# Float32 array tiles for z, scores and reads, with w_in kept in SBUF, in a fused attention and feed-forward kernel on Trainium2

## The chip, the core and the metric

The kernel runs on one core of one Trainium2 chip. The metric is device time in microseconds (us) of one execution. Before the change it was run three times: 707.71, 709.49 and 711.24 us, median 709.49 us. The profile shows one execution on core 0 whose span, from the first to the last instruction, is 706.6 us.

## The reference

Eight batches b, eight heads, 512 tokens (S), 32 states (N), head width 64 (D). Each batch is attended both ways, the two results are laid one after the other (544 rows of 512 columns), and all rows go through a feed-forward layer without gate (512 to 2048 to 512). All in float32.

```python
scores = scale * np.matmul(x, state.transpose(0, 1, 3, 2))      # 512 x 32 per head
a = softmax(scores)                                             # exp, / (sum + 1e-9)
xread = np.matmul(a, state)
scores2 = scale * np.matmul(state, x.transpose(0, 1, 3, 2))     # 32 x 512 per head
a2 = softmax(scores2)
sread = np.matmul(a2, x)
x = concat([xread, sread], axis=2)     # then tokens x (heads * 64)
h = x @ w_in
r = np.maximum(h, 0.0)
g = r * r
out = g @ w_out
```

## The kernel before, in words

The token rows need `h = a @ state @ w_in`. The kernel never forms `a @ state`; it forms `z = state @ w_in` for each head (32 states by 2048 columns), so that eight heads of 32 states make 256 rows, two groups (g = 0, 1) of 128, and `h` is a sum over these 256 rows. The state rows (`sread`) are collected over all batches in `sr` and go through the layer at the very end in a run of their own.

Full precision on the fast matrix path is had by splitting: `split` writes a rounded `hi` (type F32R, by ACT) and `lo = src - hi` (by DVE or POOL), and a product is the sum of hi*hi, lo*hi and hi*lo. A matmul whose operands are plain F32 needs no split; in the trace it is two MATMUL records for one instruction of the program.

The feed-forward layer runs in units. A unit is one 128-column piece `fc` (of 16) of the 2048 middle columns for one batch: `up(fc)` is 6 matmuls 128x512 into `ph` (line L392), then ACT takes relu (L394), DVE or ACT squares it (L398, L396), and the result is split to `g_hi`, `g_lo`; `down` is 12 matmuls 128x512 into `po` (L418), two units later. 8 batches x 16 pieces are 128 units; the state rows add 16 short units of width 256. `BOTH` sets their order: six pieces of batch 0, ten of batch 1, then the rest of both, then batches 2 to 7 whole.

Both weight matrices arrive as 64-bit words. `singles` makes float32 of them: one ACT operation (L108) and three DVE operations (L109, L113, L117) per 128x512. `wo_load` splits w_out into resident `wo_hi`, `wo_lo` (the lo part on POOL). A part of w_in (`z_part.load`, `convert`) is converted to `wf`, written to DRAM (`wd`), split (`cut`) and used for the z of four batches at once (`product`, the states of batches 0 to 3 as 128 columns): six parts by plain F32 matmuls (L191), where head pairs sit in partitions 0 to 63 and 64 to 127, the others by F32R matmuls (L203). ACT copies z out of PSUM (`z_stage`) and sends it to DRAM (`zd`); `z_fetch` brings one batch's 256 columns back by four transfers (`z_raw`, L230) and splits them to `z_hi`, `z_lo`. For batches 4 to 7 the parts of w_in are read back from `wd`. At the end the state rows read w_in from `wd` again (`wi_raw`, L624).

Attention of a batch is done in two groups of four heads: `load_t`, `cut_t`, `scores` (L288 with split operands into `pq`; L298 with plain F32 into `pst` for batches 0 and 1), a softmax along the 32 states after a DVE transpose (`soft1`, `soft1b`), and for the state rows an exp along the tokens (`e2`, L309), PE transposes (`turn`, L343), and `read` (L355).

The order of steps around the units is set by two lists (`weights`, `reads`) with due slots; each unit calls `aux` twice, and steps are taken at a rate that meets the due slots. The tile framework's scheduler then orders the instructions of each engine. PE, ACT, DVE and POOL each run their own instructions in that order; SP and ACT issue the transfers.

Of the kernel before, what the change touches and what calls it, by code (L numbers as in the profile page):

```python
# [9 lines left out]
F32 = mybir.dt.float32  # L10
# [8 lines left out]
def memory_attention_then_relu2_ffn(  # L19
# [4 lines left out]
    stT: bass.AP,  # L24
# [19 lines left out]
    B, C, S = xT.shape  # L44
    D = stT.shape[1]
# [9 lines left out]
    FW = 256  # L55
    NFCH = DF // FW
    FPC = FW // P
# [5 lines left out]
    RAW = 4  # L63
    XRAW = 2
    PLAIN_Z = 6
    PLAIN_X = 2
    BOTH = ((0, 6), (1, 10), (0, NFC), (1, NFC))
    LATE = 3

    def pool_early(early):  # L70
        return nc.gpsimd if early else nc.vector
# [3 lines left out]
    dr = ctx.enter_context(tc.tile_pool(name="dr", bufs=1, space=bass.MemoryType.DRAM))  # L75
# [6 lines left out]

    wo = [None] * NFCH
    sp_hl = const.tile([P, NG, 2, 2, 2 * N], F32R, name="sp_hl")
    nc.gpsimd.memset(sp_hl.bitcast(F32), 0.0)
    sp_f = const.tile([P, NG, 2, P + D], F32, name="sp_f")
    nc.gpsimd.memset(sp_f, 0.0)
    sr = [const.tile([P, C], F32, name=f"sr{i}") for i in range(NGB)]

    wd = [dr.tile([P, NCC, FW], F32, name=f"wd_{k}") for k in range(NFCH)]  # L90
    zd, st, z_first = {}, {}, []
    for G in range(NGB):
        for k in range(NFCH):
            zd[G, k] = dr.tile([P, NG, HG, FW], F32, name=f"zd_{G}_{k}")

# [27 lines left out]
    def z_state(G):  # L123
        if G == 0:
            raw = sb.tile([P, H, GB * N], F32, name="st_f", tag="x_hl", bufs=1)
            st["raw"] = raw
        else:
            raw = sb.tile([P, H, GB * N], F32, name="st_raw", tag="raw", bufs=RAW)
        for j in range(2):
            nc.sync.dma_start(out=raw[j * D:(j + 1) * D].rearrange("d h m -> d (h m)"), in_=stT[G])  # L130
        hi = sb.tile([P, H, GB * N], F32R, name="stz_hi", bufs=1)
        lo = sb.tile([P, H, GB * N], F32R, name="stz_lo", bufs=1)
        if G:
            split(hi, lo, raw, nc.gpsimd)
        else:
            for i in range(2):
                own = slice(i * D, (i + 1) * D)
                other = slice((1 - i) * D, (2 - i) * D)
                for v in (hi, lo):
                    nc.gpsimd.memset(v[other, i::2, :].bitcast(F32), 0.0)  # L140
                split(hi[own, i::2, :], lo[own, i::2, :], raw[own, i::2, :], nc.vector)
        st[G] = hi, lo

    def z_part(G, k, g):

        box = {}
        ccs = slice(g * NCC // NG, (g + 1) * NCC // NG)
        nq = NCC // NG

        def load():  # L150
            if G:
                box["wf"] = sb.tile([P, nq, FW], F32, name="wf", bufs=2)
                nc.sync.dma_start(out=box["wf"], in_=wd[k][:, ccs, :])
                return
            raw = sb.tile([P, nq, FW, 2], I32, name="w_raw", tag="raw", bufs=RAW)
            nc.sync.dma_start(out=raw.rearrange("p c f w -> p (c f w)"), in_=w_in[k * NG + g])
            box["raw"] = raw

        def convert():
            wf = sb.tile([P, nq, FW], F32, name="wf", bufs=2)  # L160
            singles(wf, box["raw"])
            nc.sync.dma_start(out=wd[k][:, ccs, :], in_=wf)
            box["wf"] = wf

        plain = G == 0 and k * NG + g < PLAIN_Z

        bank = dict(pool=ps_o, tag="po") if G == 0 and k == 0 else dict(pool=ps_x, tag="px")

        def cut():
            if plain:  # L170
                return
            wf = box["wf"]
            w2 = [sb.tile([P, nq, FW], F32R, name=f"w2_{i}", bufs=2) for i in range(2)]
            box["w2"] = w2
            if G == 0:
                split(w2[0], w2[1], wf, nc.vector)
                return
            for i, w in enumerate(w2):
                own = slice(i * D, (i + 1) * D)
                other = slice((1 - i) * D, (2 - i) * D)  # L180
                nc.scalar.copy(out=w[own], in_=wf[own])  # L181
                nc.gpsimd.tensor_sub(out=w[other], in0=wf[own], in1=w[own].bitcast(F32))  # L182

        def product(i):
            def run():
                own = slice(i * D, (i + 1) * D)
                pz = bank["pool"].tile([P, nq, FW], F32, name="pz", tag=bank["tag"])
                for q in range(nq):
                    h = g * HG + 2 * q + i
                    if plain:  # L190
                        nc.tensor.matmul(  # L191
                            pz[:, q, :], lhsT=st["raw"][own, h, :], rhs=box["wf"][own, q, :],
                            start=True, stop=True,
                        )
                        continue
                    st_hi, st_lo = st[G]
                    u, v = (w[:, q, :] for w in box["w2"])
                    todo = ((st_lo, u), (st_hi, u), (st_hi, v))
                    if G:
                        w = box["w2"][i][:, q, :]  # L200
                        todo = (st_lo, w), (st_hi, w)
                    for j, (a, w) in enumerate(todo):
                        nc.tensor.matmul(  # L203
                            pz[:, q, :], lhsT=a[:, h, :], rhs=w,
                            start=j == 0, stop=j == len(todo) - 1,
                        )
                if G == 0 and k == 0:
                    if g == 0 and i == 0:
                        z_first.append(sb.tile([P, NG, FW], F32, name="z_raw", bufs=2))
                    for q in range(nq):  # L210
                        at = (2 * q + i) * N
                        dst = z_first[0][at:at + N, g, :]
                        nc.scalar.copy(out=dst, in_=pz[:N, q, :])
                stage = sb.tile([P, nq, FW], F32, name="z_stage", bufs=3)
                nc.scalar.copy(out=stage, in_=pz)
                dst = zd[G, k].rearrange("p g (q i) f -> p g q i f", i=2)[:, g, :, i, :]
                nc.scalar.dma_start(out=dst, in_=stage)
            return run

        return load, convert, cut, [product(i) for i in range(2)]  # L220

    def z_fetch(b, k):
        if k or b:
            raw = sb.tile([P, NG, FW], F32, name="z_raw", bufs=2)
        at = (b % GB) * N
        if (b, k) == (0, 0):
            raw = z_first[0]
        else:
            for j in range(HG):
                nc.sync.dma_start(  # L230
                    out=raw[j * N:(j + 1) * N], in_=zd[b // GB, k][at:at + N, :, j, :]
                )
        hi = sb.tile([P, NG, FW], F32R, name="z_hi", bufs=2)
        lo = sb.tile([P, NG, FW], F32R, name="z_lo", bufs=2)
        split(hi, lo, raw, nc.vector)
        return hi, lo


    def attention(b):
        pair = []  # L240

        def pad():
            pair.extend(sb.tile([P, NG, S], F32R, name=n, bufs=2) for n in ("a_hi", "a_lo"))
            raw = sb.tile([P, NG, 2, N], F32, name="sp_raw", bufs=2)
            nc.sync.dma_start(out=raw.rearrange("p g q n -> p (g q n)"), in_=stP[b])
            for i in range(2):
                rows = slice(i * D, (i + 1) * D)
                at = slice(i * N, (i + 1) * N)
                if b < PLAIN_X:
                    nc.scalar.copy(out=sp_f[rows, :, :, at], in_=raw[rows])  # L250
                    continue
                split(sp_hl[rows, :, :, 0, at], sp_hl[rows, :, :, 1, at], raw[rows], nc.vector)

        return pair, pad, [attention_group(b, g, pair) for g in range(NG)]

    def attention_group(b, g, pair):
        CG = C // NG
        NQ = CG // P
        NJ = S // 32
        my = {}  # L260

        def load_t():
            my["t"] = sb.tile([P, NQ, S], F32, name="xt_raw", tag="xraw", bufs=XRAW)
            nc.sync.dma_start(
                out=my["t"], in_=xT[b, g * CG:(g + 1) * CG, :].rearrange("(q p) s -> p q s", p=P)
            )

# [6 lines left out]
        def cut_t():  # L274
            if b < PLAIN_X:
                return
# [228 lines left out]
    for _, _, c, ps in zs[0] + zs[1]:  # L505
        lags[ps[0]] = [(c, 2)]
# [171 lines left out]
```

## Time and profile before

| | |
|---|---|
| three runs | 707.71, 709.49, 711.24 us (median 709.49) |
| the profiled execution | span 706.6 us on core 0; its own time with what lies around the span is not recorded apart, and the median run is 2.9 us above this span |
| busy | PE 669.8, DVE 452.2, ACT 398.3, POOL 199.3 us |
| mean granted TensorE clock | 0.973 |
| transfers | 90.58 MB, HBM read 60.03 MB, written 29.88 MB |

The span divides in two. Up to about 125 us DVE converts the weights, the transfer engines are busy for eight to nine tenths, and PE waits between pieces and is at times granted half its clock. From 125 us on PE is busy nearly without a gap until the last outputs leave. A busy PE is not by that a PE at its peak: durations of single matmuls overlap, and the distance from one start to the next is what one costs in a row of them.

### The profile page before, as it was taken

How to read it: one execution, taken by the hardware profiler on the slowest of the kernel's cores; microseconds unless marked ns; L12 is line 12 of the kernel's file. 1: busy time of each engine (PE TensorE's matmuls, PEld its weight loads, DVE VectorE, ACT ScalarE, POOL GpSimd, SP SyncE). 2: the span in 40 equal slices, each digit the busy share in tenths (PEclk: the TensorE clock that was granted, in tenths of full speed). 3: DMA queues.
4: the chain of work that ended last, by engine and by line, in shares of the span. 5: the costliest groups of instructions: out<-in, count | busy, mean ns of one | idle time of the engine just before them, and what ended most of it. 6: DMA issues, size and time to landing. Idle time of an engine off the chain costs nothing.

```text
span 706.6 us, 9753 instructions
## 1 busy us (share of the span) xinstructions
PE 669.8 (95%) x3152; PEld 551.6 (78%) x3152; DVE 452.2 (64%) x757; ACT 398.3 (56%) x727; POOL 199.3 (28%) x181
## 2 busy tenths in 40 slices
PE   4688789999999999999999999999999999999997
PEld 2355668778888888888888878888888888888996
DVE  4859999758456944447945794797944445443553
ACT  3767687567565863467735653665654344332442
POOL 2314433345443540053403240344242022000000
PEclk8589999999999999999999999999999999999999
DMA  8898899435363542344423312412241112100421
GB/s 276 270 315 283 258 306 315 131 97 153 98 202 122 166 149 62 102 135 120 135 78 120 87 48 74 139 58 90 89 150 61 30 31 90 31 16 0 130 80 32
DMA packets 74548, 90.58 MB, mean 128 GB/s; under 512 B 7680, under 2 KB 57600, under 8 KB 74496
## 3 DMA queue, kind: packets, MB, share of 16 engines
q1 hardware_dynamic: 56896, 72.90, 32.9%
q10 hardware_dynamic: 17600, 17.04, 7.1%
q8 instruction: 25, 0.41, 0.3%
q14 instruction: 27, 0.22, 0.1%
HBM read 60.03 MB, written 29.88 MB: 127 GB/s over the span
## 4 chain that ended last, share of the span: by engine, by line
PE 79%; DVE 8%; DMA 6%; issue 2%; ACT 2%; SPq 1%; POOL 0%; DVEq 0%; ACTq 0%; POOLq 0%
PE po L418 47%; PE ph L392 25%; PE pz L203 3%; DMA wo_raw<-w_out 2%; PE pr L355 2%; DMA sp_raw<-stP 2%; PE pq L288 1%; PE pt L343 1%; DVE wf L117 1%; DVE wf L113 1%; DVE z_lo L98 1%; DVE g_lo L98 1%; DMA zd<-z_stage 1%; DMA xt_raw<-xT 1%; DVE wf L109 1%
## 5 line engine op out<-in xcount | busy, mean ns | idle before, releaser
L418 PE MATMUL po<-wo_hi,g_hi 128*128 128x512 f32 x544 | 217.3, 400 | 0.6 <-ACT g_hi L97 0.5
L418 PE MATMUL po<-wo_lo,g_hi 128*128 128x512 f32 x544 | 215.0, 395 | 0.0
L398 DVE TENSOR_TENSOR ph<-ph,r 128x512 f32<-128x512 f32 (+1 forms) x134 | 89.1, 665 | 169.1 <-ACT r L394 168.9
L394 ACT ACTIVATE r<-ph 128x512 f32<-128x512 f32 (+1 forms) x144 | 82.1, 572 | 171.0 <-PE ph L392 169.6
L418 PE MATMUL po<-wo_hi,g_lo 128*128 128x512 f32 x544 | 152.2, 392 | 0.0
L418 PEld LDWEIGHTS po<-wo_hi,g_hi 128*128 128x128 f32 x544 | 103.9, 191 | 22.4 <-ACT g_hi L97 2.0
L418 PEld LDWEIGHTS po<-wo_lo,g_hi 128*128 128x128 f32 x544 | 103.9, 191 | 19.5
L418 PEld LDWEIGHTS po<-wo_hi,g_lo 128*128 128x128 f32 x544 | 101.5, 189 | 21.1 <-issue 1.0
L98 DVE TENSOR_TENSOR g_lo<-ph,g_hi 128x512 fp32r<-128x512 f32 (+1 forms) x144 | 94.4, 656 | 36.3 <-ACT g_hi L97 27.7
L97 ACT CAST g_hi<-ph 128x512 fp32r<-128x512 f32 (+1 forms) x144 | 81.0, 563 | 57.9 <-DVE ph L398 51.7
L392 PE MATMUL ph<-a_hi,z_hi 128*128 128x512 f32 x256 | 81.4, 399 | 2.6 <-DVE nm L306 1.5
L392 PE MATMUL ph<-a_lo,z_hi 128*128 128x512 f32 x256 | 80.1, 392 | 0.0
L392 PE MATMUL ph<-a_hi,z_lo 128*128 128x512 f32 x256 | 80.0, 394 | 0.0
L98 POOL TENSOR_TENSOR xn_hl<-xn_raw,xn_hl 128x1024 fp32r<-128x1024 f32 x16 | 38.9, 2432 | 138.0 <-ACT xn_hl L97 71.2
L182 POOL TENSOR_TENSOR w<-wf,w 64x512 fp32r<-64x512 f32 x32 | 43.0, 1343 | 74.9 <-ACT w L181 69.8
L392 PEld LDWEIGHTS ph<-a_hi,z_hi 128*128 128x128 f32 x256 | 47.6, 190 | 15.2 <-DVE g_lo L98 2.1
L392 PEld LDWEIGHTS ph<-a_hi,z_lo 128*128 128x128 f32 x256 | 48.5, 190 | 10.4
L392 PEld LDWEIGHTS ph<-a_lo,z_hi 128*128 128x128 f32 x256 | 48.2, 189 | 10.5 <-issue 0.3
L98 POOL TENSOR_TENSOR xt_hl<-xt_raw,xt_hl 128x1024 fp32r<-128x1024 f32 x12 | 28.9, 2406 | 75.4 <-ACT xt_hl L97 43.7
L98 DVE TENSOR_TENSOR z_lo<-z_raw,z_hi 128x512 fp32r<-128x512 f32 x64 | 47.9, 750 | 0.3 <-DMA wd<-wf 0.3
L97 ACT CAST z_hi<-z_raw 128x512 fp32r<-128x512 f32 x64 | 39.2, 615 | 1.3 <-DMA wd<-wf 0.8
L98 POOL TENSOR_TENSOR wo_lo<-wof,wo_hi 128x512 fp32r<-128x512 f32 x16 | 25.2, 1578 | 51.4 <-ACT wo_hi L97 51.4
(97 smaller groups left out, 833.7 us busy)
## 6 DMA issues: line engine op xcount, KB each, us to landing
zd<-z_stage ACTq DMA_DIRECT2D x64, 256.0 KB, 3.2
z_raw<-zd SPq DMA_DIRECT2D x252, 64.0 KB, 2.4
xt_raw<-xT SPq DMA_DIRECT2D x16, 512.0 KB, 3.8
w_raw<-w_in SPq DMA_DIRECT2D x16, 512.0 KB, 5.3
wo_raw<-w_out SPq DMA_DIRECT2D x16, 512.0 KB, 5.8
xn_raw<-xn SPq DMA_DIRECT2D x16, 512.0 KB, 3.9
out<-sum SPq DMA_DIRECT2D x32, 256.0 KB, 2.5
wd<-wf SPq DMA_DIRECT2D x16, 256.0 KB, 3.7
```

Source lines behind the costliest of these rows:

```text
L97: nc.scalar.copy(out=hi, in_=src)
L98: eng_lo.tensor_sub(out=lo, in0=src, in1=hi.bitcast(F32))
L109: nc.vector.tensor_scalar(out=bits, in0=bits, scalar1=3, scalar2=0x7FFFFFF8, op0=ALU.logical_shift_left, op1=ALU.bitwise_and,)
L113: nc.vector.scalar_tensor_tensor(out=bits, in0=high, scalar=-0x80000000, in1=bits, op0=ALU.bitwise_and, op1=ALU.bitwise_or,)
L117: nc.vector.scalar_tensor_tensor(out=bits, in0=low, scalar=29, in1=bits, op0=ALU.logical_shift_right, op1=ALU.bitwise_or,)
L182: nc.gpsimd.tensor_sub(out=w[other], in0=wf[own], in1=w[own].bitcast(F32))
L203: nc.tensor.matmul(pz[:, q, :], lhsT=a[:, h, :], rhs=w, start=j == 0, stop=j == len(todo) - 1,)
L355: nc.tensor.matmul(pr[:, q].rearrange("p i c -> p (i c)"), lhsT=my["e"][:, t, q].rearrange("p i n -> p (i n)"), rhs=my["xn"][:, t, q].rear ...
L392: nc.tensor.matmul(ph, lhsT=w, rhs=v, start=i == 0, stop=i == len(todo) - 1)
L394: nc.scalar.activation(r, ph, AF.Relu)
L398: nc.vector.tensor_mul(out=ph, in0=ph, in1=r)
L418: nc.tensor.matmul(po[t], lhsT=g, rhs=w, start=i == 0 and j == 0, stop=i == last and j == 2)
```

## The change

w_in is converted once into a resident float32 tile `wi` (128 partitions by 4 by 2048: partitions 0 to 63 hold heads 0 to 3, 64 to 127 heads 4 to 7), and stays there; `wd`, `zd`, `z_stage`, `z_raw` and the states of four batches (`stT`) are gone. z of one batch is made when its units come near (`z_piece`): for up to four units at a time, 8 plain F32 matmuls of 64 rows by 32 columns of the array (4 column places j, 2 row halves g), into two PSUM banks; ACT and DVE split the result from PSUM to `z_hi`, `z_lo`. Scores are 8 such matmuls per batch, for all batches, and the result stays in PSUM through both softmaxes. Reads are 32 plain F32 matmuls of 128 rows by 32 columns and 64 wide per batch; the division by the sum moves from `e2` to the 8 small copies into `sr` (DVE). A batch is handled whole, not in two groups, except the softmax of batch 0. `load_w` and `convert_w` work on one queue of 16 pieces of w_in and 16 of w_out, five raw buffers instead of four. The PSUM pool `ps_x` has one buffer of two banks instead of two of one. `BOTH` becomes eight pieces of batch 0, twelve of batch 1, then the rest; `LATE` is 2. POOL keeps `wo_lo`, `a_lo` of batches 1 to 7 and the two softmax operations of batch 1.

```diff
-    RAW = 4
-    PLAIN_Z = 6
-    PLAIN_X = 2
-    BOTH = ((0, 6), (1, 10), (0, NFC), (1, NFC))
-    LATE = 3
+    ZC = 4
+    RAW = 5
+    BOTH = ((0, 8), (1, 12), (0, NFC), (1, NFC))
+    LATE = 2
...
-    ps_x = ctx.enter_context(tc.tile_pool(name="ps_x", bufs=2, space=bass.MemoryType.PSUM))
+    ps_x = ctx.enter_context(tc.tile_pool(name="ps_x", bufs=1, space=bass.MemoryType.PSUM))
...
+    wi = const.tile([P, HG, DF], F32, name="wi")
...
-    def z_part(G, k, g):
-    def z_fetch(b, k):
+    def z_piece(b, units, first):
+        def run():
+            c, at = divmod(units[0], ZC)
...
+            width = len(units) * P
+            cols = slice(units[0] * P, units[0] * P + width)
+            if first:
+                pz = [ps_o.tile([P, S], F32, name=f"pz{g}", tag="po")[:, :width] for g in range(NG)]
+            else:
+                both = ps_x.tile([P, NG, S], F32, name="pz", tag="px")
+                pz = [both[:, g, :width] for g in range(NG)]
+            for j in range(HG):
+                for g in range(NG):
+                    rows = slice(g * D, (g + 1) * D)
+                    nc.tensor.matmul(
+                        pz[g][j * N:(j + 1) * N], lhsT=state[b][rows, j, :],
+                        rhs=wi[rows, j, cols], start=True, stop=True,
+                    )
+            if not first:
+                split(z_hi[:, :, dst], z_lo[:, :, dst], both[:, :, :width], nc.vector)
+                return
...
         def scores():
+            pst = ps_x.tile([P, NG, S], F32, name="pst", tag="px")
+            for j in range(HG):
+                for g in range(NG):
+                    rows = slice(g * D, (g + 1) * D)
+                    nc.tensor.matmul(
+                        pst[j * N:(j + 1) * N, g, :], lhsT=state[b][rows, j, :],
+                        rhs=my["t"][rows, j, :], start=True, stop=True,
+                    )
...
         def read():
+            pr = ps_x.tile([P, NG, S], F32, name="pr", tag="px")
+            for g in range(NG):
+                for t in range(NT):
+                    for j in range(HG):
+                        h = g * HG + j
+                        nc.tensor.matmul(
+                            pr[j * N:(j + 1) * N, g, :D], lhsT=my["e"][:, g, t, j * N:(j + 1) * N],
+                            rhs=my["n"][:, t, h * D:(h + 1) * D], start=t == 0, stop=t == NT - 1,
+                        )
...
+                    nc.vector.tensor_scalar_mul(
+                        sr[b // GB][at:at + N, c:c + D], pr[own, g, :D], my["s2"][own, g:g + 1]
+                    )
...
+    def z_due():
+        while pieces:
+            first, b, cover = pieces[0]
+            if slot[0] < 2 * (first - 2) or ("wi", cover[-1]) in queue[converted[0]:]:
+                break
+            pieces.pop(0)
+            z_piece(b, cover, first < 2)()
...
     def first(fc):
-        raw = sb.tile([P, NCC, P], F32, name="wi_raw", tag="raw", bufs=RAW)
-        nc.sync.dma_start(out=raw, in_=wd[k][:, :, i * P:(i + 1) * P])
...
-        split(w_hi, w_lo, raw, nc.vector)
+        split(w_hi, w_lo, wi[:, :, fc * P:(fc + 1) * P], nc.vector)
```

How the instructions stand, at the places that the prediction speaks of. First PE in the middle of the program. In the order before, z is made in F32R matmuls 128x256 that use the whole array; `w_0` is a part of split w_in, `stz` the split states of four batches, and the rows around are one unit's `up` and `down`.

```order
L418 MATMUL po_2099<-wo_hi_1164,g_lo 128x512
L203 MATMUL pz<-w_0_2888,stz_hi 128x256
L203 MATMUL pz<-w_0_2888,stz_lo 128x256
L418 MATMUL po_2096<-wo_hi_1164,g_hi 128x512
L418 MATMUL po_2096<-wo_lo_1165,g_hi 128x512
L418 MATMUL po_2097<-wo_hi_1164,g_hi 128x512
L418 MATMUL po_2097<-wo_lo_1165,g_hi 128x512
L392 MATMUL ph<-a_hi,z_hi 128x512 x2
```

All of them have the shape of the whole array. Now the same engine in the order after, at a z piece of batch 2 (`sp_raw` is the batch's state, plain F32, and `32x512 x5` are five matmuls with 32 output rows each):

```order
L300 MATMUL po_1670<-wo_hi,g_lo 128x512
L130 MATMUL pz<-wi,sp_raw 32x512 x5
L300 MATMUL po_1667<-wo_hi,g_hi 128x512
L300 MATMUL po_1667<-wo_lo,g_hi 128x512
L300 MATMUL po_1668<-wo_hi,g_hi 128x512
L274 MATMUL ph<-a_hi,z_hi 128x512 x2
```

The other three of that piece's eight stand in the two units that follow, as `L130 MATMUL pz<-wi,sp_raw 32x512 x2` and, 31 rows further on, alone. Counted over the whole order, the 37 pieces of z stand in 55 groups and the 8 scores in 8, with matmuls of full shape in between. The next fence is the last of the three of that piece.

```order
L300 MATMUL po_1670<-wo_hi,g_lo 128x512
L130 MATMUL pz<-wi,sp_raw 32x512
L300 MATMUL po_1667<-wo_hi,g_hi 128x512
L300 MATMUL po_1667<-wo_lo,g_hi 128x512
L300 MATMUL po_1668<-wo_hi,g_hi 128x512
```

A piece that is one step in the code has become three short stretches of PE here.

Then DVE early in the program, up to the eighth `g_lo`, which ends the input of the eighth unit. Before:

```order
L113 SCALAR_TENSOR_TENSOR wof<-wo_raw,wof 128x512
L117 SCALAR_TENSOR_TENSOR wof<-wo_raw,wof 128x512
L98 TENSOR_TENSOR z_lo<-z_raw,z_hi 128x512
L98 TENSOR_TENSOR w_1_985<-wf,w_0_984 128x512
L109 TENSOR_SCALAR wf<-wf 128x512
L113 SCALAR_TENSOR_TENSOR wf<-w_raw,wf 128x512
L117 SCALAR_TENSOR_TENSOR wf<-w_raw,wf 128x512
L98 TENSOR_TENSOR g_lo<-ph,g_hi 128x512
L109 TENSOR_SCALAR wof<-wof 128x512
L98 TENSOR_TENSOR g_lo<-ph,g_hi 128x512
```

Up to here DVE has begun 24 conversions. After, up to the same `g_lo`:

```order
L93 TENSOR_SCALAR wof<-wof 128x512
L97 SCALAR_TENSOR_TENSOR wi<-wi_raw,wi 128x4x128
L82 TENSOR_TENSOR g_lo<-ph,g_hi 128x512
L97 SCALAR_TENSOR_TENSOR wof<-wo_raw,wof 128x512
L101 SCALAR_TENSOR_TENSOR wi<-wi_raw,wi 128x4x128
L101 SCALAR_TENSOR_TENSOR wof<-wo_raw,wof 128x512
L93 TENSOR_SCALAR wi<-wi 128x4x128
L93 TENSOR_SCALAR wof<-wof 128x512
L97 SCALAR_TENSOR_TENSOR wi<-wi_raw,wi 128x4x128
L82 TENSOR_TENSOR g_lo<-ph,g_hi 128x512
```

It has begun 29 of the 32 conversions by then. The splits of w_in (`w_1`) are gone, and z_lo is rarer; conversions have moved into their place.

More of the change, by code (lines that the diff above doesn't have):

```diff
@@ L120, in singles @@
         )
[L123 to L142, printed above, removed]
@@ L144, in z_part @@
-    def z_part(G, k, g):
[L146 to L153, printed above, removed]
-                return
[L155 to L220, printed above, removed]
@@ L222, in z_fetch @@
-    def z_fetch(b, k):
[L223 to L236, printed above, removed]
+    zt = {}
@@ L239, in attention @@
+    state = {}
     def attention(b):
-        pair = []
+        NJ = S // 32
+        pair, my = [], {}
+        halves = [slice(g, g + 1) for g in range(NG)] if b == 0 else [slice(0, NG)]
         def pad():
             pair.extend(sb.tile([P, NG, S], F32R, name=n, bufs=2) for n in ("a_hi", "a_lo"))
[L244 to L260, printed above, removed]
+            state[b] = sb.tile([P, HG, N], F32, name="sp_raw", bufs=3)
+            nc.sync.dma_start(out=state[b].rearrange("p j n -> p (j n)"), in_=stP[b])
         def load_t():
[L263 to L266, printed above, removed]
+            my["t"] = sb.tile([P, HG, S], F32, name="xt_raw", bufs=1)
@@ L282, in scores @@
[L282 to L297 removed]
+            my["n"] = sb.tile([P, NT, C], F32, name="xn_raw", bufs=1)
@@ new lines, in read @@
+            for g in range(NG):
+                for j in range(HG):
+                    c = (j * NG + g) * D
+                    own = slice(j * N, (j + 1) * N)
+                    nc.vector.tensor_scalar_mul(
+                        sr[b // GB][at:at + N, c:c + D], pr[own, g, :D], my["s2"][own, g:g + 1]
+                    )
+        steps = dict(
+            pad=pad, load_t=load_t, scores=scores, exps2=exps2, load_n=load_n, turn=turn, read=read
+        )
+        return pair, steps, [soft(gs) for gs in halves]
@@ L516, in order @@
[L516 to L530 removed]
+        _, w, softs = attentions[b]
@@ new lines, in memory_attention_then_relu2_ffn, with load_next, convert_next @@
+    loaded, converted = [0], [0]
+    def load_next():
+        if loaded[0] < len(queue):
+            load_w(*queue[loaded[0]])
+            loaded[0] += 1
+    def convert_next():
+        convert_w(*queue[converted[0]])
+        converted[0] += 1
+        load_next()
+    pieces = []
+    now = 0
+    for b, fcs in parts:
+        i = fcs[0]
+        while i <= fcs[-1]:
+            new = at[i] == now + i - fcs[0]
+            n = ZC
+            if new:
+                n = 1 if i < 2 else 2
+            cover = range(i, i + n)
+            pieces.append((now + i - fcs[0], b, cover))
+            i += n
+        now += len(fcs)
```

297 lines of the change are left out of this document (114 added, 183 removed).

## The prediction

> **What bounds the kernel now.** I read the engine shares of the page first, then its 40 slices, then the chain that ended last.
>
> ```profile
> PE 669.8 (95%) x3152; PEld 551.6 (78%) x3152; DVE 452.2 (64%) x757; ACT 398.3 (56%) x727; POOL 199.3 (28%) x181
> PE   4688789999999999999999999999999999999997
> DVE  4859999758456944447945794797944445443553
> PEclk8589999999999999999999999999999999999999
> PE 79%; DVE 8%; DMA 6%; issue 2%; ACT 2%; SPq 1%; POOL 0%; DVEq 0%; ACTq 0%; POOLq 0%
> ```
>
> The reader should see two stages. In the first seven slices (17.7 us each) PE has holes, and its granted clock falls to 0.5 in one of them, while DVE stands at nine tenths. From the eighth on PE is full. Work that leaves DVE, ACT, POOL or the transfers after about 125 us therefore gives no time back; only PE's own work counts there, and before it DVE's. The next windows bear this out: three of DVE, one of POOL, one of `g_lo` on DVE alone, one of all engines with PE first. Behind the stretch and its length stand busy time and instructions, then granted clock, DMA share and GB/s.
>
> ```profile
> 0.00:9.20 9.20, 0.00 (x0) 1.00 0.75 253
> 9.20:60.00 50.80, 40.39 (x76) 0.73 0.87 279
> 60.00:103.40 43.40, 41.65 (x67) 0.88 0.89 299
> 0.00:103.40 103.40, 35.60 (x34) 0.82 0.87 285
> 0.00:103.40 103.40, 5.23 (x8) 0.82 0.87 285
> 150.00:200.00 50.00, 50.00 (x244) 42.13 (x244) 35.31 (x62) 34.73 (x62) 28.42 (x22) 1.00 0.46 143
> ```
>
> At 103.4 us the eighth `g_lo` is done (x8): eight units have had their `up`, six their `down`. I cut the kernel there and count PE's work behind it.
>
> **PE's work behind the cut, before.** What a matmul costs in a row of them:
>
> ```profile
> 301.45 1.82 PE po L418 x8
> 688.46 1.43 PE ph L392 x12
> 172.12 0.60 PE L343 MATMUL pt<-ident,e 128*128 128x128 f32 x4
> 172.48 0.36 PE L203 MATMUL pz<-w,stz_lo 128*128 128x256 f32 x1
> ```
>
> That is 0.2275 us for 512 columns, 0.119 for 256, so 0.000424 us per column and some 0.01 fixed; and 0.09 for a 128-wide transpose (0.36 between the two starts, by four). The layer has 128 units of 18 and 96 last `down` matmuls, 2400 at 0.2275 = 546.0, and 192 at 0.119 = 22.9: 568.9 us. Less the 8 x 6 + 6 x 12 = 120 that lie ahead of the cut (27.3), 541.6 remain, in both kernels.
>
> ```profile
> L203 PE MATMUL pz<-w,stz_hi 128*128 128x256 f32 x144 | 33.7, 292 | 2.0 <-DVE w L98 2.0
> L203 PE MATMUL pz<-w,stz_lo 128*128 128x256 f32 x104 | 29.0, 294 | 6.5 <-ACT w L97 2.5 <-ACT e L309 2.4 <-ACT z_stage L215 1.5
> L355 PE MATMUL pr<-xn_hl,e_hl 128*128 128x256 f32 x128 | 19.7, 282 | 0.0
> L288 PE MATMUL pq<-xt_hl,sp_hl 128*128 128x512 f32 x48 | 14.6, 391 | 0.7 <-ACT z_stage L215 0.7
> L343 PE MATMUL pt<-ident,e 128*128 128x128 f32 x64 | 11.2, 272 | 0.0
> ```
>
> Of z, 176 of the 248 F32R matmuls stand behind the cut by the order: 20.9. Scores 48 x 0.2275 = 10.9, reads 128 x 0.119 = 15.2, transposes 64 + 8 at 0.09 = 6.5. Sum 53.5; 103.4 + 541.6 + 53.5 = 698.5, and 8 of the 706.6 are left for idle time and the tail. The account closes, so I use it for the kernel after.
>
> **PE's work behind the cut, after.** The change lets 8 float32 matmuls of 64 rows by 32 columns stand in the array together. The trace has plain F32 matmuls on half the rows, at half clock: eight records that use both halves, and four that use one.
>
> ```profile
> 14.97 2.08 PE L191 MATMUL pz<-wf,st_f 64*128 64x256 f32 x8 [3.95 <-DVE wf L117]
> 40.91 2.04 PE L191 MATMUL pz<-wf,st_f 64*128 64x256 f32 x4 [0.68 <-DVE wf L117]
> 14.90:17.20 2.30, 2.08 (x8) 0.50 1.05 378
> 42.00:42.10 0.10, 0.10 (x2) 0.50 1.01 410
> ```
>
> Twice the work in the same time (2.08 against 2.04): row halves run fully side by side. Column places are not in this trace. The bounds are 8 at once and 2 at once; I take 8, because the one kind of tiling that is shown costs nothing. The Trainium skill's page "TensorE: Matmul & The Clock Gate" (section "Part 3: Packing small matmuls — row/col tiling") gives 10.6 times for 16 tiles and 2.38 for three column tiles, less than the count; that two halves gave all of 2 is better than its ratio. By the page's 0.66 to 0.79 the tiles would take, as an estimate, 56 to 68 us here and not the 44.8 below, and the sum would be 745 to 757.
>
> A record of n columns takes two passes (four of 256 columns one after another, at half clock, fit 2.04 with the tail of the last), and a plain F32 matmul has two records. So one group costs 4 x 512 x 0.000424 = 0.87 us at 512 wide and 0.43 at 256, if it holds one matmul or eight. This is where the order costs: behind the cut z stands in 42 groups of 512 and 7 of 256, since many pieces are cut in 5, 2 and 1. That is 36.5 + 3.0 = 39.5, where whole pieces would need 25. Scores of six batches: 5.2.
>
> Each group is a change of array shape and back. The nearest row is a pair of 64-row matmuls between full ones at full clock (last row: granted 1.00):
>
> ```profile
> 49.63 0.39 PE L418 MATMUL po<-wo_hi,g_lo 128*128 128x512 f32 x1
> 49.95 1.13 PE L191 MATMUL pz<-wf,st_f 64*128 64x256 f32 x4
> 51.01 1.98 PE L298 MATMUL pst<-xt_raw,sp_f 128*128 128x512 f32 x4
> 49.90:50.00 0.10, 0.10 (x2) 1.00 0.84 338
> ```
>
> From 49.63 to 49.95 is 0.32 where 0.2275 would do: 0.09 going in. From 49.95 to 51.01 is 1.06 where four records take 0.87: 0.19 coming out. 0.28 a group, times 55 groups (49 of z, 6 of scores): 15.4.
>
> Reads: 32 matmuls of 64 columns per batch, 64 records of 0.054 us of columns. At least 0.87 us a batch, four column places at once; at most 64 x 0.09 = 5.8, the transposes' pace one after another. The ends lie far apart and no row is near: weights are a quarter as wide as the transposes', but there are 64 of them. I take their geometric middle, 2.2, and 0.28: 2.5 a batch, 20 for eight, where 15.2 stood before. Transposes stay at 6.5.
>
> The bank pair `ps_x` has one buffer. In five batches a z piece or a transpose stands 3.6 us of PE behind the scores, and the scores must first be read out:
>
> ```profile
> L303 DVE STREAM_TRANSPOSE q<-st 128x512 f32<-128x512 f32 x12 | 8.4, 699 | 0.2
> L305 DVE TENSOR_REDUCE nm<-st 128x1 f32<-128x512 f32 x12 | 7.7, 643 | 0.0
> L309 ACT ACTIVATE e<-st,nm 128x512 f32<-128x512 f32 x12 | 8.7, 726 | 1.6 <-DVE nm L306 1.4
> ```
>
> Two of each: 1.4 + 1.3 + 1.5 = 4.2 us, and more if DVE is behind. 0.6 to some 2 us, five times; I take 4 in all (0 to 10). PE in its order stands still in that wait, `up` and `down` included.
>
> **The start.** Here DVE decides, and the order says what it has to do before the eighth `g_lo`.
>
> ```profile
> 0.00:103.40 103.40, 14.72 (x24) 0.82 0.87 285
> 0.00:103.40 103.40, 16.92 (x24) 0.82 0.87 285
> 0.00:103.40 103.40, 18.85 (x23) 0.82 0.87 285
> 8.57 0.67 ACT L108 ACTIVATE wf<-w_raw 128x512 f32<-128x512 f32 x1 [3.90 <-DMA w_raw<-w_in]
> 4.93 6.09 PE L298 MATMUL pst<-xt_raw,sp_f 128*128 128x512 f32 x8 [4.93 <-DMA xt_raw<-xT]
> DVE wof L109 <- ACT wof L108: 6.2, 2, 4.1
> ```
>
> The first three rows are L109, L113, L117: 50.5 us for 71 conversion operations, 0.71 each. The other 31.5 of DVE's 82.0 are 49 operations of 512 elements and 22 small ones, some 0.58 and 0.13. After, there are 29 + 55 = 84 conversion operations (60), 40 of 512 counted by width (23) and 12 small (2): 85. So DVE has no less to do for eight units: what z in DRAM cost it is taken up by conversions moved ahead. POOL holds DVE up, as this pair shows (most L117 steps take 0.68):
>
> ```profile
> 88.80 1.33 POOL L98 TENSOR_TENSOR a_lo<-at,a_hi 128x512 fp32r<-128x512 f32 x1 [1.64 <-ACT a_hi L97]
> 88.90 1.78 DVE L117 SCALAR_TENSOR_TENSOR wf<-w_raw,wf 128x512 int32<-128x512 int32 x1
> ```
>
> It has about 27 us of work in that stretch (13 `wo_lo`, two softmax steps, one `a_lo`) where 35.6 stood; I give 1 for that. DVE starts earlier, since the first w_in piece is now second in SP's queue, ahead of x: a transfer in that place landed at 4.93, its ACT step took 0.67, so 5.6 against 9.2. The transfers keep up: 29 conversions of 0.52 MB and 3 MB of x are 18 MB, 64 us at the 285 GB/s of this stretch. Of the other 12 us in which DVE was idle, 6.2 were waits for w_out; with five raw buffers and w_in no longer written and read back I keep 4. The cut comes at 5.6 + 84 + 4 = 94 us; 88 if POOL's hold falls by half, 103 if all waits stay.
>
> What is removed behind the cut is priced at nothing, with PE as its cover: 64 `z_stage` copies and transfers, 252 `z_raw` transfers of four per fetch on SP's queue, the `w` splits on ACT and POOL, the `wi_raw` loads. The scores that ACT and DVE now read from PSUM and the 64 small copies into `sr` fall under the same cover.
>
> **Sum.** 94 + 541.6 + 39.5 + 5.2 + 15.4 + 20 + 6.5 + 4 and the tail behind the last matmuls,
>
> ```profile
> 700.94 0.61 PE L418 MATMUL po<-wo_hi,g_lo 128*128 128x512 f32 x2
> ```
>
> 5.2 us (two matmuls at 0.2275 from 700.94 on, to 706.6, the end of the span), give 731.4 against 706.6. The median of the three runs is 2.9 above the span: 734 us. In short: 9 us won at the start, 37 lost in PE's stage, in which there was no slack.
>
> **Rivals.** (1) Column places run one after another, only row halves together. Then z's groups behind the cut need 110, scores 21, reads 5.8 + 0.28 a batch, 48.6: 848 us. For it: no row shows column places side by side. Against it: the halves are told apart by the hardware at no cost. (2) A record with its weight load cannot follow another faster than a transpose does, 0.09 us. Then a full group of 16 records takes 1.44, not 0.87: 25 such groups add 14, the 256-wide ones 3.5, reads 28.6, so 780. For it: each tile brings its own weights. Against it: the eight records above kept up with the array. (3) The other side: changes of shape cost nothing and the reads run at their columns' pace, because the next matmul fills the array while the last tile drains. That takes off 15.4 and 8 x 1.63 = 13, giving 705; it decides once these two together fall by 28 with the cut at 94, or by 22 with the cut at 88, which gives 699. For it: matmuls of one shape overlap completely in the rows above. Against: the 0.28 is measured. (4) No change, 706 to 713: the same, in part. That the tiles do not come about at all is rival (1).
>
> **How the numbers follow.** Forecast (slower, 713 to 765) 0.45; rival (1) 0.10; (2) 0.10; (3) 0.27; (4) 0.08. The likeliest is the forecast, 734. Its own range comes from the cut (88 to 103), reads (7 to 49), stalls (0 to 10) and 0.28 on 55 groups: 713 to 765. The range 697 to 772 takes in rival (3) with an early cut and leaves out (1) and (2), 2 in 10. A measurement here tells about 0.5% (3.5 us) from no change. Faster 0.27, same 0.08, slower 0.65.
>
> **What the profile after would show.** PE groups of `pz` with 16 records in about 0.9 us and, cut in three, about 0.9 each: right. 16 records in 3.5 us or more: rival (1); in 1.4: rival (2). A start-to-start excess at the edges of a `pz` group near 0.28, or near nothing, tells (3). `pr` of one batch within 1 to 6 us. The eighth `g_lo` near 94 us, DVE 85 to 90 us busy by then. Behind it PE full except for waits on `pst`. The prediction is wrong if PE behind the cut has less than 605 us of work, or if the eighth `g_lo` comes before 75 us.

## The result, and the profile after

Four runs of the changed kernel: median 759.02 us (758.24 to 759.76), against 709.19 us (707.71 to 711.24) for the kernel before in the same session. The ratio is 1.0718, 95% interval 1.0685 to 1.0750: slower by 49.8 us. The direction was forecast and the time lies in the stated range, but the change is twice the forecast one (734 us, 24.5 slower). The profiled execution took 759.13 us with a span of 757.3. Of the runs below, one execution of hp_z took 2279 us and the profile fell on it, which is why that kernel stands there twice.

First the page: engine shares, the slices of PE, DVE and the clock (18.9 us each), and the chain that ended last.

```profile
PE 687.0 (91%) x3896; PEld 504.7 (67%) x3896; DVE 399.4 (53%) x624; ACT 282.1 (37%) x479; POOL 44.3 (6%) x31
PE   1477979999969999989998999899998999999997
DVE  5999953343566724483346433562447543334543
PEclk9999989999979999999999999999999999999999
PE 77%; DVE 10%; issue 7%; ACT 2%; DMA 2%; POOL 0%; SPq 0%; ACTq 0%; POOLq 0%; DVEq 0%
```

DVE's stretch at nine tenths ends some 30 us earlier than before, and PE is no longer full behind it: there are a six and several eights among its nines, and the chain spends 10% on DVE and 7% on issue (8 and 2 before).

The same cut as in the prediction, at the end of the eighth `g_lo`. The windows show `g_lo` on DVE up to the cut, all of DVE up to the cut, and all engines behind it (PE first; then granted clock, DMA share, GB/s).

```profile
0.00:88.40 88.40, 5.37 (x8) 0.98 0.67 233
0.00:88.40 88.40, 80.65 (x133) 0.98 0.67 233
88.40:757.30 668.90, 636.45 (x3619) 472.92 (x3617) 318.76 (x493) 232.54 (x391) 20.45 (x11) 0.98 0.10 34
```

The cut came at 88.4 us (predicted 94). Behind it PE stands still for 32 of 668.9 us by its busy time, and the clock of 0.98 is some 13 us of lost speed (11.8 of them while PE ran, summed over the stretches of half clock). The waits behind the cut (total, times, longest) name 27.4 us, 26.7 of them in these three lines:

```profile
PE po L300 <- ACT g_hi L81: 19.7, 9, 5.7
PE pt L232 <- DVE z_lo L82: 4.2, 1, 4.2
PE pz L130 <- ACT e L185: 2.8, 1, 2.8
```

The second and third are waits for the one bank pair `ps_x`: the transposes `pt` wait until DVE has read a piece of z out of it, and a piece of z until ACT has read the scores. With one of 0.4 us (`pt` behind `sr`) they are 7.4 us. The first is of another kind.

The timeline rows of PE at a whole piece of z, at a piece cut down to one matmul, and at the reads of a batch (start, duration, then what; a matmul is two records):

```profile
330.74 0.40 PE L300 MATMUL po<-wo_lo,g_hi 128*128 128x512 f32 x1
331.06 1.09 PE L130 MATMUL pz<-wi,sp_raw 64*32 64x512 f32 x16
332.08 0.73 PE L274 MATMUL ph<-a_hi,z_hi 128*128 128x512 f32 x2
...
285.93 1.04 PE L130 MATMUL pz<-wi,sp_raw 64*32 64x512 f32 x2
286.90 0.50 PE L300 MATMUL po<-wo_hi,g_hi 128*128 128x512 f32 x1
287.24 0.40 PE L300 MATMUL po<-wo_lo,g_hi 128*128 128x512 f32 x1
...
200.05 1.10 PE L244 MATMUL pr<-xn_raw,e_t 128*32 128x64 f32 x64
201.08 0.73 PE L274 MATMUL ph<-a_hi,z_hi 128*128 128x512 f32 x2
```

Eight matmuls (16 records) take 1.02 us to the next start, one matmul 0.97. So all eight tiles work side by side, and each part of a broken piece pays as a whole piece does. With 0.09 going in (0.32 from 330.74 instead of 0.2275) and 0.11 on the next rows (0.34 from 286.90), a 512-wide group costs 1.22 us. The 64 records of the reads take 1.03.

Last, one of the places where PE stands still, with the three engines together, behind the scores of one batch (not every row between is shown):

```profile
320.70 1.08 PE L274 MATMUL ph<-a_hi,z_hi 128*128 128x512 f32 x4
321.71 1.09 PE L167 MATMUL pst<-xt_raw,sp_raw 64*32 64x512 f32 x16
322.90 1.25 DVE L200 STREAM_TRANSPOSE q<-pst 128x1024 f32<-128x1024 f32 x1 [3.31 <-PE pst L167]
323.29 0.63 PE L274 MATMUL ph<-a_lo,z_hi 128*128 128x512 f32 x2
323.76 0.62 PE L274 MATMUL ph<-a_hi,z_lo 128*128 128x512 f32 x2
324.02 0.60 ACT L276 ACTIVATE r<-ph 128x512 f32<-128x512 f32 x1 [5.68 <-PE ph L274]
324.08 1.19 DVE L182 TENSOR_REDUCE nm<-pst 128x2 f32<-128x1024 f32 x1
324.21 0.62 PE L274 MATMUL ph<-a_lo,z_hi 128*128 128x512 f32 x2
325.19 1.20 DVE L207 TENSOR_REDUCE m<-q 128x32 f32<-128x1024 f32 x1
326.31 0.69 DVE L280 TENSOR_TENSOR ph<-ph,r 128x512 f32<-128x512 f32 x1
327.03 0.59 ACT L81 CAST g_hi<-ph 128x512 fp32r<-128x512 f32 x1 [1.49 <-DVE ph L280]
327.67 0.79 PE L300 MATMUL po<-wo_hi,g_hi 128*128 128x512 f32 x1 [2.83 <-ACT g_hi L81]
328.26 0.63 PE L300 MATMUL po<-wo_lo,g_hi 128*128 128x512 f32 x1
...
327.70:330.70 3.00, 3.00 (x7) 2.42 (x8) 2.79 (x6) 2.70 (x6) 0.00 (x0) 0.51 0.00 0
```

Two units' `ph` stand next to each other around the scores, with no `po` between them. The first unit's last `ph` (from 323.29) gives way to the next at 323.76; four more `ph` (0.9 us) are all that PE has until the `po` that needs this very unit. Relu, square and cast take 1.9 us at the least, and here 3.7, because the square (L280) stands in DVE's queue behind three softmax operations of 1024. PE waits 2.83 us, and then its matmuls start 0.43 apart instead of 0.23: the window's clock is 0.51. The same 2.83 us comes back at 408.89, 491.51 and 572.78.

### The profile page after: what moved, and what is told of

It is laid out like the page before. It is cut to its first block, busy times and chain, and to the rows that moved or that the text cites. A ratio compares the mean times of both kernels' runs of the same rounds, so it can differ in the third digit from the quotient of the medians.

```text
span 757.3 us, 9704 instructions
## 1 busy us (share of the span) xinstructions
PE 687.0 (91%) x3896; PEld 504.7 (67%) x3896; DVE 399.4 (53%) x624; ACT 282.1 (37%) x479; POOL 44.3 (6%) x31
## 4 chain that ended last, share of the span: by engine, by line
PE 77%; DVE 10%; issue 7%; ACT 2%; DMA 2%; POOL 0%; SPq 0%; ACTq 0%; POOLq 0%; DVEq 0%
PE po L300 46%; PE ph L274 23%; PE pz L130 6%; DMA wi_raw<-w_in 2%; DVE wof L97 1%; DVE wi L97 1%; DVE q L200 1%; DVE wi L101 1%; DVE m L207 1%; DVE nm L182 1%; PE pr L244 1%; DVE wof L101 1%; PE pst L167 1%; ACT g_hi L81 1%; PE pt L232 1%
## 5 line engine op out<-in xcount | busy, mean ns | idle before, releaser
L300 PE MATMUL po<-wo_hi,g_hi 128*128 128x512 f32 x544 | 224.3, 412 | 21.7 <-ACT g_hi L81 21.7
L300 PE MATMUL po<-wo_lo,g_hi 128*128 128x512 f32 x544 | 218.7, 402 | 0.0
L280 DVE TENSOR_TENSOR ph<-ph,r 128x512 f32<-128x512 f32 (+1 forms) x134 | 88.8, 666 | 196.6 <-ACT r L276 196.3
L300 PE MATMUL po<-wo_hi,g_lo 128*128 128x512 f32 x544 | 155.9, 396 | 0.0
L300 PEld LDWEIGHTS po<-wo_lo,g_hi 128*128 128x128 f32 x544 | 105.5, 194 | 21.6
L274 PE MATMUL ph<-a_hi,z_hi 128*128 128x512 f32 x256 | 84.5, 414 | 6.8 <-ACT a_hi L81 3.4
L130 PE MATMUL pz<-wi,sp_raw 64*32 64x512 f32 (+2 forms) x592 | 56.1, 583 | 25.6 <-ACT wo_hi L81 9.7
L82 DVE TENSOR_TENSOR z_lo<-pz,z_hi 128x1024 fp32r<-128x1024 f32 (+2 forms) x39 | 39.9, 1028 | 35.8 <-ACT z_hi L81 35.8
L81 ACT CAST z_hi<-pz 128x1024 fp32r<-128x1024 f32 (+2 forms) x39 | 33.3, 860 | 39.4 <-PE pz L130 39.4
L82 POOL TENSOR_TENSOR a_lo<-at,a_hi 128x1024 fp32r<-128x1024 f32 x7 | 17.1, 2436 | 469.6 <-ACT a_hi L81 393.4
L130 PEld LDWEIGHTS pz<-wi,sp_raw 64*32 64x32 f32 x592 | 9.3, 110 | 47.4 <-issue 15.7
L82 POOL TENSOR_TENSOR wo_lo<-wof,wo_hi 128x512 fp32r<-128x512 f32 x16 | 22.5, 1406 | 65.6 <-ACT wo_hi L81 65.6
```

What stands on the lines that cost most here:

```text
L81: nc.scalar.copy(out=hi, in_=src)
L82: eng_lo.tensor_sub(out=lo, in0=src, in1=hi.bitcast(F32))
L130: nc.tensor.matmul(pz[g][j * N:(j + 1) * N], lhsT=state[b][rows, j, :], rhs=wi[rows, j, cols], start=True, stop=True,)
L274: nc.tensor.matmul(ph, lhsT=w, rhs=v, start=i == 0, stop=i == len(todo) - 1)
L280: nc.vector.tensor_mul(out=ph, in0=ph, in1=r)
L300: nc.tensor.matmul(po[t], lhsT=g, rhs=w, start=i == 0 and j == 0, stop=i == last and j == 2)
```

## The experiments

"The groups of z" below are counted in the order of PE: 55 in the changed kernel for 37 pieces. "Reserve" is the work that PE has in its order between the last `ph` of a unit and the first `po` that needs this unit, by the rows' prices. The changed kernel has four units with a reserve of 0.9 us, exactly those of the four waits of 2.83 us.

**Squares on ACT (sq_act).**

```diff
-            if units[0] < 10:
+            if True:
                 nc.scalar.activation(ph, r, AF.Square)
```

> The squares of the units from the eleventh on go to ACT instead of DVE; nothing else is edited. Theory one (the added 47 us over the sum of instructions is PE standing still and then running at half clock, because DVE, which works in order, waits 3.3 us for the scores and then runs three 1024-wide softmax operations of 3.6 us ahead of the square that the next unit needs): the square no longer stands behind them, the ten longest waits of PE on g_hi (19.7 us) and most of the half clock behind them go, so 20 to 35 us less, 724 to 739 us. Theory two (the single bank pair of z, scores, transposes and reads is what PE waits for): the bank is released by the same instructions as before, so within 5 us of 759. Theory three (the array tiles themselves bring the half clock): the granted clock in the stretches with z stays, less than 10 us gained.

755.74 us, 3.3 less. Theory one, DVE's softmax ahead of the square, falls as the whole cause. Its mechanism is there: the four waits went from 2.83 to 1.40 us, and no half clock followed them. The waits, and the window behind one of them:

```profile
PE po L300 <- ACT g_hi L81: 13.2, 8, 5.7
326.61 0.51 PE L300 MATMUL po<-wo_hi,g_hi 128*128 128x512 f32 x1 [1.40 <-ACT g_hi L81]
326.70:329.70 3.00, 3.00 (x13) 2.46 (x14) 2.80 (x7) 3.00 (x7) 0.00 (x0) 1.00 0.22 93
```

The reserve of 0.9 us is still there, against a chain of 2.3. And the new order cuts z into 63 groups, eight more (the expectation of hp_sq below says 61, without the two first pieces), which at 1.22 us each would be some 10 us and takes back most of what the waits and the clock gave.

**Softmax in halves (halves).**

```diff
-        halves = [slice(g, g + 1) for g in range(NG)] if b == 0 else [slice(0, NG)]
+        halves = [slice(g, g + 1) for g in range(NG)]
```

> The softmax of every batch goes in two 512-wide halves, as that of the first batch does already; squares stay on DVE. Theory one: DVE still waits for the scores, but a square has at most 1.2 us of softmax ahead of it at a time where the scheduler lets it in between, so each of the 2.8 us waits shrinks by 1 to 2 us, while the doubled instruction count adds some 2 to 3 us of DVE work a batch: 740 to 757 us. Theory two (bank): the exponentials that release the bank come no earlier, so 755 to 765. If the scheduler keeps both halves together, no change.

760.32 us. The four waits stayed, at 2.95 us, and z had 61 groups. Theory two forecast this time too, but the wait was again `po` on `g_hi`; the wait for the bank (`pz` on `e`) was 2.9 us, once. So the bank is not the cause of the four waits.

**Pieces kept together by a critical section (whole), and twice (double).**

```diff
+            with tc.tile_critical():
                 for j in range(HG):          # double: for k in range(2), for j ...
                     for g in range(NG):
```

> The eight array-tile matmuls of a piece of z are kept together, so z is computed in 37 groups instead of 55; nothing else is edited. If the number of groups sets the cost of z (each group pays its width and the change of shape, whether it holds one matmul or eight): 18 groups less at 0.87 to 1.23 us, mostly 512 wide, so 11 to 18 us less, 741 to 748 us. If a broken group costs in proportion to its matmuls (a single one 0.2 us): 18 changes of shape at 0.28, so 4 to 6 us less, 753 to 755 us. Theory one's waits on DVE stay where they are in either case.

> As the kernel with whole pieces, but each piece's eight matmuls are issued twice, the second writing the same numbers again: 37 more groups of eight in one shape, without a further change of shape (28 of 512, 7 of 256, 2 of 128 columns). Compared with the kernel with whole pieces: side by side, 28 x 0.87 + 7 x 0.43 + 2 x 0.22 = 28 us more. If the four column places of a group took their turn, 112 us more; if the two row halves, 56 us more. If array tiles are what brings the half clock, more than 28: up to 56.

Whole: 763.10 us, 4 more than the changed kernel where 4 to 18 less were forecast. Its section made PE wait at the start for transfers that have nothing to do with z (the waits up to 140 us):

```profile
PE pz L131 <- DMA wo_raw<-w_out: 37.1, 3, 17.8
```

The cut came at 111.0 us, 22.6 later. Behind it the kernel took 648.2 us instead of 668.9, its clock was 0.99, and none of the four waits was left; but PE still stood still for 36 of these 648.2 us by its busy time, 9.4 of it in 21 short waits of `pz`. Double: 793.48, 30.4 more than whole, where 28 stood for all tiles side by side, 56 and 112 for places that take turns, and up to 56 for tiles that bring the half clock; its clock was 0.983 to whole's 0.984. That leaves side by side alone.

**Pieces kept together by priority (hp_z, hp_z2), and squares on ACT with it (hp_sq).**

```diff
+            with tc.high_priority():
                 for j in range(HG):
                     for g in range(NG):
```

> The eight array-tile matmuls of every piece of z get priority in the scheduler, so they stand together on PE without the barrier that the kernel of kept-together pieces had: 37 groups instead of 55, squares on DVE as in the changed kernel. The kernel with kept-together pieces took 648 us behind the end of the eighth unit's g_lo (changed kernel 669) but reached that point 22 us later. Theory four (groups of z cost by their number, and the order that goes with whole groups leaves PE other work behind the scores): the start of the changed kernel (88 us) and 640 to 648 us behind it, 729 to 738 us. Theory one alone (DVE's softmax in front of the square): the waits of 2.8 us stay, only the groups' 18 x 0.9 to 1.2 us go, 738 to 743 us. If broken groups cost nothing extra: 755 to 760.

> Both together: pieces of z kept whole by priority, and all squares on ACT. Squares on ACT alone gave 3 us with six more groups of z than the changed kernel (61 against 55), which at 1.2 us would be 7 us, so by itself it is worth some 10 us in waits and clock. If the two add up: 8 to 12 us under the kernel with whole pieces by priority, 719 to 730 us. If whole pieces have removed the same waits already: the same time as that kernel within 3 us.

> The kernel with whole pieces of z by priority once more, unchanged, for its profile. Its order on PE has, between the last ph matmul of a unit and the first po that needs that unit, never less than 1.7 us of other PE work by the rows of the changed kernel, where the changed kernel's order has four units (those behind the scores of batches 2 to 5 in it) with 0.9 us. Theory five (that reserve decides the four waits of 2.83 us): none of these four waits in the profile, PE's clock 0.99 or more behind the start, 709 to 713 us. Theory one (DVE's softmax in front of the square decides them, whatever PE has in reserve): four waits of 2 us or more remain.

710.88 us and, for the second time, 710.82 (ratio to the kernel before in the same session 1.0051, 1.0036 to 1.0066, so 3.4 us over it): 48 us less than the changed kernel, by the order of the same instructions. Theory four had forecast 729 at the least, since it took the stretch behind the cut from whole, where PE stood still for 36 us; here it does for 11, out of 616.5 behind a cut at 92.2. The two longest groups of waits behind the cut, the window from 96 us on, and the place behind the scores that answers to the one above (not every row between is shown):

```profile
PE po L301 <- ACT g_hi L81: 1.5, 3, 0.7
PE ph L275 <- ACT z_hi L81: 1.2, 1, 1.2
...
96.00:708.70 612.70, 601.86 (x3580) 461.94 (x3580) 308.71 (x485) 227.05 (x385) 18.73 (x9) 1.00 0.10 37
...
298.88 1.09 PE L168 MATMUL pst<-xt_raw,sp_raw 64*32 64x512 f32 x16
300.46 0.62 PE L275 MATMUL ph<-a_lo,z_hi 128*128 128x512 f32 x2
300.93 0.39 PE L301 MATMUL po<-wo_hi,g_hi 128*128 128x512 f32 x1
301.18 0.60 ACT L277 ACTIVATE r<-ph 128x512 f32<-128x512 f32 x1 [4.31 <-PE ph L275]
302.36 1.20 DVE L208 TENSOR_REDUCE m<-q 128x32 f32<-128x1024 f32 x1
302.55 0.40 PE L301 MATMUL po<-wo_lo,g_hi 128*128 128x512 f32 x1
303.48 0.69 DVE L281 TENSOR_TENSOR ph<-ph,r 128x512 f32<-128x512 f32 x1
304.18 1.10 PE L301 MATMUL po<-wo_hi,g_lo 128*128 128x512 f32 x4
304.20 0.59 ACT L81 CAST g_hi<-ph 128x512 fp32r<-128x512 f32 x1 [0.79 <-DVE ph L281]
305.11 0.40 PE L301 MATMUL po<-wo_hi,g_hi 128*128 128x512 f32 x1
```

DVE does the same here: the square waits from 301.8 to 303.48 behind the softmax. But PE has a whole unit's `po` in reserve (302.55 to 305.1) and never notices. That decides for theory five against theory one. Behind its cut the kernel takes 52.4 us less than the changed one, while the cut comes 3.8 later. Of the 52.4, waits are 21.6 (27.4 against 5.8) and half clock 11.8 (none is left here while PE runs); of the other 19, z's own matmuls are 15.8 (45.0 against 29.2, from one start on PE to the next, with gaps and half clock taken out), although the reads stand in 13 groups here instead of 8. hp_sq, 714.43 us, is 3.5 over hp_z: in its order three of the reserves of 0.9 us are back, with three waits of 1.39 us (4.2 together). Squares on ACT do not add up with whole pieces.

**Broken pieces with the reserve (split6).**

```diff
+                    with tc.high_priority() if j < 3 else nullcontext():
                         nc.tensor.matmul(pz[g][...], ...)
```

> Six of a piece's eight matmuls get priority, the last two do not, so z is again in 54 groups (changed kernel 55, whole pieces 37), but PE's order keeps at least 1.7 us of other work behind every unit, as with whole pieces. This parts the two things that whole pieces changed at once. If the number of groups carries the 48 us between the changed kernel and the one with whole pieces: close to 759, over 745. If the reserve (waits and the half clock behind them) carries it: close to 711, under 720. If both do, by the groups' own rows: 17 groups more at 0.87 to 1.23 us, so 15 to 21 us over 711: 726 to 732 us, and the remaining 27 to 33 us is waits and clock.

737.77 us: 21.3 under the changed kernel with one group of z fewer (54), and 27.0 over whole pieces. Both matter. The waits behind its cut at 88.2:

```profile
PE pz L131 <- DVE z_lo L82: 7.4, 1, 7.4
PE pt L233 <- DVE z_lo L82: 3.2, 1, 3.2
PE ph L275 <- ACT a_hi L81: 2.1, 1, 2.1
PE po L301 <- ACT g_hi L81: 2.0, 3, 1.6
```

The four waits behind the scores are gone, as theory five says. The 27 us over whole pieces are above the 15 to 21 expected: 17.8 us of waits are left behind the cut instead of 5.8, most of them for the bank pair, the first of them 7.4 us at 99 us, in which a piece of z stood in PE's queue until DVE had read the piece before out of it. Counted by starts as above, z costs 13.8 us more than with whole pieces (43.0 against 29.2); the waits add 12.0 and the half clock 5.3, and the cut comes 4.0 earlier, which makes 27.1.

**One matmul more in each group (hp_one).**

```diff
-                for j in range(HG):
-                    for g in range(NG):
+                for j, gs_ in [(0, (0,))] + [(j, range(NG)) for j in range(HG)]:
+                    for g in gs_:
```

> Whole pieces by priority, and the first of a piece's eight matmuls is issued once more ahead of the eight (it writes the same numbers): nine in a group instead of eight, no change of shape more. If a group lasts as long as its busiest place in the array (the prediction's step: one matmul costs as much as eight): 28 x 0.87 + 7 x 0.43 + 2 x 0.22 = 28 us over the kernel with whole pieces, about 739 us. If cost goes by the number of matmuls: an eighth of that, 3 to 4 us, 714 to 715 us.

734.09 us, 23.3 over hp_z2: the ninth matmul, on a place of the array that has one already, costs nearly what the eight cost together. A group lasts as long as its busiest place. PE's rows:

```profile
237.64 1.90 PE L131 MATMUL pz<-wi,sp_raw 64*32 64x512 f32 x18
239.47 0.74 PE L275 MATMUL ph<-a_hi,z_hi 128*128 128x512 f32 x2
```

1.83 against 1.02 is 0.81 us, for 28 pieces 22.7.

**Tries at a faster version (hp_down, late, late_sq).** In the first, `down` is written ahead of `up`. In the other two conversions are queued on DVE behind the last `g_lo`; late_sq squares 24 units on ACT.

```diff
+        with tc.issue_after(last_lo[0].ins) if last_lo else nullcontext():
             convert_w(*queue[converted[0]])
```

> Whole pieces by priority, and in the written order of a unit its down projection (po) stands ahead of the up projection two units later, instead of behind it. A try at a faster version: PE has the same 37 groups; if the two reserves of 1.7 us that are left are what still costs time, no gain, since they stay; if a longer way from up to down helps elsewhere, up to 4 us less than 711; if the softmax steps come late by it, up to 10 us more.

> Whole pieces of z by priority, and the conversions of the weights stand in DVE's queue behind the g_lo of the unit in whose slot they are written, instead of being drawn ahead of it. In the kernel with whole pieces DVE is busy without a break up to the end of the eighth unit's g_lo (92 us), 64 us of it on conversions, most of all 32 tiles; here 50 instead of 86 conversion instructions stand ahead of that point, 29 us less by those instructions' means of 0.54 to 0.95 us. If DVE's throughput sets the start: the point comes 15 to 29 us earlier; the conversions follow in a stretch where DVE is four tenths busy, so most of it stays, 690 to 700 us, faster than the kernel before. If the start hangs on the chain of PE, ACT and loads instead: 705 to 712.

> The same, and ACT squares the first 24 units instead of the first 10, which takes 14 x 0.69 = 10 us from DVE where the conversions now come later. If DVE's lack of time behind the start brings waits of PE there: 2 to 6 us under the kernel with late conversions alone. If not: the same within 2 us, or 1 to 3 us more, as squares on ACT gave with whole pieces (3.5 us more).

714.25, 710.22 and 710.09 us (the last 1.0016 times the kernel before, 0.9994 to 1.0038). hp_down has its cut 2 us later and no wait less that counts. In late the eighth `g_lo` came 7.6 us earlier, not 15 to 29, and next to nothing came of it: the stretch behind it took 623.5 us instead of 616.5, since 19 fewer of the layer's matmuls (4.3 us) were done by then. What holds the start is not shown by these runs; PE's longest waits up to the cut name a conversion on DVE and ACT's `a_hi`:

```profile
PE pz L131 <- DVE wi L101: 19.8, 4, 10.2
PE ph L275 <- ACT a_hi L81: 9.6, 1, 9.6
```

No version beat the kernel before; the best is level with it.

## Why the prediction was off by 25 us

By its own sum, predicted and measured, in us of the span:

| term | predicted | measured |
|---|---|---|
| cut | 94 | 88.4 |
| layer behind the cut | 541.6 | 537.3 (139 of its matmuls lie ahead of the cut, not 120) |
| z, scores and changes of shape | 39.5 + 5.2 + 15.4 = 60.1 | 49 groups and 6 scores at 1.22 (512) and 0.79 (256): 64.0 |
| reads | 20 | 8 x 1.25 = 10 |
| transposes, tail | 11.7 | 7.0 + 5.6 = 12.6 |
| PE standing still | 4 | 27.4 |
| half clock behind it | 0 | 11.8 |
| not named | 0 | 5.8 (what is left) |
| sum | 731.4 | 757.3 |

**The term that was mis-sized** is "I take 4 in all (0 to 10)", for PE standing still, and the step that failed is "Behind it PE full except for waits on `pst`": it counted only the wait for the one bank pair. The waits for this pair came to 7.4 us, inside its 0 to 10, and only 2.8 of them were for the scores to be read out. What it put at nothing is `po` waiting for ACT's cast of a unit just computed: nine waits with 19.7 us, the four of 2.83 behind the scores and one of 5.7 right behind the cut among them. The granted clock that falls behind such gaps cost another 11.8, and it was put at nothing too. These 31.5 us are more than the whole miss of 25.9, since reads, cut and layer came out 20 better. Part of the missing step could have been done from the order alone: the reserve of 0.9 us can be counted there, and relu, square and cast had their durations in the trace (1.9 us at the least here). I had read the order for how many pieces of z are cut, not for what PE is left with when they are.

That 759 lies inside the forecast's own 713 to 765 is luck. The upper end of that range owed most to the reads, at up to 49 us, and they took 10; its stalls ended at 10, and 27.4 were measured.

**Right:** that PE's own work and waits decide behind the cut; that eight tiles stand side by side and a group costs one or eight the same (0.97 and 1.02 us; hp_one, double); the change of shape, 0.28 predicted, 0.35 measured with the 0.11 on the next rows; that broken pieces cost: by the prediction 14.5 us and the edges, by the starts in hp_z2 15.8, and the edges on the rows beside them come on top.

**The reads** cost half of the "geometric middle": the lower end, 0.87 a batch and the edges, was right. That is rival (3)'s second half; its first half was wrong, edges are not free. Rivals (1) and (2) fall with the 1.02 us.

The Trainium skill's page "TensorE: Matmul & The Clock Gate" (section "Part 3: Packing small matmuls — row/col tiling"), by which the time was to be 745 to 757 us, an estimate, comes near the measured 759, but not by its rule: packing here gave nearly the full count (eight in 1.02 us, one in 0.97), and the time was lost elsewhere, as hp_z2 with the same tiles shows.

**The start**: DVE's 85 us were 80.7, and the idle time 7.7 instead of 9.6. The "8 x 6 + 6 x 12 = 120" matmuls of the layer ahead of the cut are 128 in the windows before (48 `ph`, 80 `po`) and 139 after, 1.8 and 4.3 us.

**Open:** why the order of the changed kernel has both units' `ph` ahead of every `po` at four places. The kernels with whole pieces and squares on DVE that left the start as it was (whole, hp_z, hp_one, hp_down) kept the reserve, and split6 kept it with broken ones; which choice of the scheduler decides it was not tried. The bank pair was not doubled either, so its 7.4 us are put down to it by the trace alone. Nor was the wait of 5.7 us behind the cut tried by itself; the rows there show ACT and DVE on conversions and copies ahead of the cast.

## What to carry to other kernels

Where a change puts new matmuls into PE's queue, look in the order at what stands between a result and its first use there, and set it against the chain of the other engines (here 0.9 us against 2.3 to 3.7): DVE working off a softmax is free while a unit of other work is in reserve, and costs its wait and the clock behind it when not. Small array tiles are paid by the group, so give a group priority and keep it whole; and see in the order what that does to the work around it, since here it moved the reserve too. When the sum of instructions closes but the stalls are a guess, the range belongs on the stalls.

## What the runs showed of the hardware

- **The clock falls behind short gaps.** Behind PE's four gaps of 2.83 us in the changed kernel the granted clock was 0.51 to 0.54 for the next 3 us. From 200 us on it fell to a half within 2 us behind six more gaps of this length: one of 2.82 us in the changed kernel (215.0), one of 2.81 in sq_act (213.2) and the four of 2.95 in halves. Behind the gaps of 1.40 us (sq_act, four times) and 1.61 there it stayed at 1.00. No fixed limit follows from this: behind one gap of 2.83 at 90.2 us in hp_z2 it stayed at 1.00 as well, and in the start, where gaps lie closer together, a half followed one of 1.75 us (hp_sq, 84.8 us). The Trainium skill's page "TensorE: Matmul & The Clock Gate" (section "Part 1: The HAM clock gate (the "warmup" mystery)") says that the clock halves after an idle window of about 3.4 us, and that the window runs free. By that a gap of 2.83 us could not halve it; here it did, and the measurement decides.
- **Tiles of 64 by 32** keep up with the array: eight matmuls 512 wide in 1.02 us to the next start, one in 0.97, and a ninth on a place already taken adds 0.81. Sixty-four records of 128x32 weights with 64 columns take 1.03 us, 16 ns each, far below the 90 ns of a 128-wide transpose.
